# A scan and a mixture of adapters on one core: new orders for all engines, the sigmoid table first, 14 warm-up transposes

## The chip, the core and the metric

The kernel runs on one core of one Trainium2 chip. A core has five engines, each with an instruction queue of its own that is worked off strictly in order: TensorE (PE: matrix products and transposes), VectorE (DVE), ScalarE (ACT), GpSimd (POOL) and SyncE (SP), which here only issues DMAs. They meet through semaphores. Data comes from and goes to HBM through 16 DMA engines. The metric is the time of one execution in microseconds on the device; three runs of the kernel before gave 208.76, 209.05 and 209.07 us, median 209.05.

## What is computed

Two arrays `a` and `b` of 8 x 6400 x 128 (float32) are scanned along their second axis, and the result `x`, seen as 51200 rows of 128, passes through a mixture of eight low-rank adapters, of which each row takes two:

```python
h = a[:, t] * h + b[:, t]; x[:, t] = h          # for t in 0 .. 6399, h = 0 at the start

logits = x @ w_gate                              # 128 -> 8
topk = the two largest logits of each row
w = softmax of these two
out = x + sum over the two e of w_e * (x @ A[e]) @ B[e]     # 128 -> 16 -> 128
```

26.2 MB are read for `a`, as much for `b`, and 26.2 MB are written.

## The kernel before

The 51200 rows are cut into 100 chunks of 512 rows (`C`, line 148). `a` and `b` come by load DMAs (line 271) in pieces of one chunk (256 KB) for the first and the last four chunks and of four chunks (1 MB) between (`LOADS`, line 12), into four buffers `a_tm` and four `b_tm` of four chunks each. A buffer is loaded anew as soon as the transposes of its old chunks are done.

A chunk then passes through these steps; the letter is the one that stands for the step in the orders below:

- `a` on PE (line 308): four transposes of `a` into PSUM bank 0; `a` on ACT (line 321): the copy to `a_st`. There is one bank, so the next chunk's transposes wait for this copy.
- `b` on PE (line 308): four transposes of `b` into bank 1 or 2, where VectorE reads them.
- `s` on DVE (line 372): the scan along time, `x = a*x + b`, into `xT` in float16; the start value is the last column of the chunk before.
- `z` on PE (line 392): `x` times `A` and `w_gate` (128 x 136) for blocks of 128 rows; `z` on ACT (line 399): the copy of two or three blocks to `zl`.
- gating for a group of 1 to 6 chunks (`GROUPS`, line 14): `1 2 3 4 6` on DVE (lines 423 to 434) find the largest and the second largest logit, `5` on POOL (432) takes their difference, `u` and `v` on ACT (437, 439) its sigmoid with both signs, `p q r` on POOL (443 to 447) make the weights.
- `m` (line 469): the products with the weights, on POOL or DVE (`MU`, a letter for each chunk: `p` or `d`).
- `t` on PE (line 477): four transposes of them; `t` on ACT or DVE (lines 482, 483): the copy to `zwT` (`TE`, a letter for each chunk: `a` or `d`).
- `d` on PE (lines 491, 492): identity times `x` plus the products with `B`; `o` on ACT (line 502): the copy to `outt`.
- `o` on SP (line 528): the store DMA, one chunk (256 KB) for the first and last four chunks, two (512 KB) between: 54 stores.

On SP, `x` and `y` are the loads of `a` and of `b`; the very first `y` is issued by ACT, and so are the three loads of the constants (`c`, line 237). `w` on PE (line 241) are warm-up transposes of the identity matrix, whose results nobody uses; there are 30 (`WARM`), 16 of them ahead of the first chunk and the rest spread among the first chunks. `i` on ACT (line 238) is one sigmoid of a column, there to have its table loaded.

No scheduler decides the order: `ORDER` (lines 20 to 49) has one string for each engine, and `arrange` takes the steps of each letter in sequence. The waits follow from that order and the dependences. The numbers `dur=` beside the steps serve the search that made the strings; nothing on the chip reads them.

Of the kernel before, what the change touches and what calls it, by code (L numbers as in the profile page):

```python
# [18 lines left out]
WARM = 30  # L19
ORDER = {  # L20
    "pe": (
        "wwwwwwwwwwwwwwwwawwwwbawbwwzwzwwbazzwazabwwazabtzbwadbzazbzatbazbzazzbazbadbzatzbaztbadzztbazzbabztd"
        "bazdzbadzbazzbatzbaztzbadzbatdbzatzzdabbtzadtdzbabtzzadtdbadtzbatzbzabtdzzabdtazzdtbazdzbatzbzadtbaz"
        "dtbabdaztbzazdtazbzdbtadzztabztzddatbzzdtbabztdabdtzazbztazbddtadbzatdzztabdtabzbtadzztabzdtbzdatzdb"
        "atdbaztdazbzdaztbzdtbadztbzatzdbazdztbabdtazdtabzztbatzdadtzdzatbbadtzzdbtdazbtdzatdbazbztabzddtbzaz"
        "tddaztbbadtdzaztbbtzzdatadtbbdztdzabzzdabtzzatddzztdatbbtaddtzbzatdbatdazdtzabbtzadtbdzzbdaztzdaztdt"
        "zabtdabbztddztzbazdtbztzaddtbaztdbbztzadztzdtzdtdtzddttdtddttdtddtdd"
    ),
    "act": (
        "cyccaaizzzazvazavuuaatzazozazzatazzavzuazzaovuzaztaztazztaozzaztoavuzzazoazzatzazoazzoatzazuvoaotzaz"  # L30
        "tzaooazoozatuzazzvoazzaooazzatzzaooauzvzazoaooaztazzaozzoauzzozazvotoazzoazoaozaztazooazzuvaotazzoaz"
        "oazozzaooazoauvtzazoazozzaoozuaovzzatozzazaooazoaztvzazoauzzaooaotzotzavoozazoauzzatozozatzoatzouaov"
        "oazzztzaaoouozzaozzaovzzaoozzaotaozazoaoauvztaoozzoatozzazoozaztazvuooaztozztoazozzaotouuavozvzzaztz"
        "otootoutvzzoovuotovuootoooo"
    ),
    "dve": (
        "iscs1234s162346smmss1s2s132s34s46s6sss1s2s3s4s6sss1sst2s3s4st6s1ssts2t34sst6s1tsts23s4ststst1s263sst"
        "s4tst16tsstststss2346tstsstst1sts1t223t4s36s4ststststs1236st4ststsst6123t4tsmsms6tstss12st34ss6tstss"
        "1t2346tstsststttsstst123t4s6stssst12t34m6stssst1st1223344st66sts1m213m24346m6mtmt12m3m4tm6tmt"
    ),  # L40
    "pool": (
        "cc5q5ppqrr55qprmqpmrmm5qprmmmmmm5pqrmmmm5mmpqrmm5mmmmpqrmmm5mmmqprmmmmm5mqprmmmmmm5pqrmmm5mmmpqrm5mm"
        "mmm5qprmmmmpqrmm5mmmqprmm5mmmmqprmmmmmmm5pqrmmmm5mpqrmmmmm55mqpprmqr5q5prqpr5pqr"
    ),
    "sp": (
        "xxyyxxxyyxyxyxoyxyxyooxyxoyooxyyxxyooxoyyoxoxyoxyooxooyoxooyxoyooxyooxyooxoyoxoyooxoyooyyxxooxyyxooo"
# [4 lines left out]
    "aaaaaaadadaaddadddadddaddddadddaddadddddaddddadddadddaaddadaaddadddddddadddadaddadaaddaddaaaaddaddad"  # L51
)
MU = (
    "ddppppppppppppppppppppppppppppppppppppppppppppppppppppddpppppppppppppppppppppppppppdpppppppddddddddd"
# [80 lines left out]
def bass_associative_scan_2x2__then__mixture_of_adapters_kernel(  # L135
# [24 lines left out]
    seg_of = [s for s, m in enumerate(SEGMENTS) for _ in range(m)]  # L160
# [3 lines left out]
    with ExitStack() as stack:  # L164
# [53 lines left out]
        def dma_sem(key):  # L218
# [4 lines left out]
        o_ms = P.add("pool", "c", [], lambda: eng["pool"].memset(ident_f[:, :], 0.0), dur=0.2)  # L223
# [5 lines left out]
            ), dur=0.3,  # L229
# [8 lines left out]
        P.add("act", "i", [o_id], lambda: eng["act"].activation(tiny[:, :], ident_f[:, 0:1], ACTF.Sigmoid), dur=1.6)  # L238
        o_ih = P.add("dve", "i", [o_id], lambda: eng["dve"].tensor_copy(ident_h[:, :], ident_f[:, :]), dur=0.25)
        for k in range(WARM):  # L240
            w = P.add("pe", "w", [o_id], lambda: eng["pe"].transpose(ps[:, BANK_O[0], 0:128], ident_f[:, :], ident_f[:, :]),  # L241
                      dur=0.218 if k < 12 else 0.109)
            user[BANK_O[0]] = [w]
# [7 lines left out]
        tm_user = [[[None] * 4 for _ in range(NL)] for _ in range(2)]  # L251
        loads = []
        s, pos = 0, 0
        for n in LOADS:
            m = SEGMENTS[s]
            assert all(SEGMENTS[s + k] == m for k in range(n)) and pos % 4 + n * m <= 4
            loads.append((s, n, m, pos // 4 % NL, pos % 4))
            for k in range(n):
                place[s + k] = (pos // 4 % NL, pos % 4 + k * m)
            pos += n * m  # L260
            s += n
        assert s == len(SEGMENTS)

        def load(s, n, m, sl, q):
            P.at = first[s]
            for w, (o_l, tile, src) in enumerate(((o_la, a_tm, af), (o_lb, b_tm, bf))):
                e = "act" if s == 0 and w else "sp"
                old = [tm_user[w][sl][q + k] for k in range(n * m)]
# [7 lines left out]
                for k in range(n):  # L276
                    o_l[s + k] = op

        def landed(tile, s):

            sl, q = place[s]
            m = SEGMENTS[s]
            return tile[sl][:, q : q + m, :].rearrange("p h (j d) -> p (h j) d", d=D)


        o_A, o_B, o_ae, o_sc = {}, {}, {}, {}
        ast_user = [None] * NA
        x_user = [[] for _ in range(NX)]
        turn = {"a": 0, "b": 0, "z": 0}

        def front(s):
            m = SEGMENTS[s]
            sl, q = place[s]
            c0 = first[s]
            if m == 2 and turn["b"] % 2:
                turn["b"] += 1
            bk = bank(BANK_B, turn["b"])
            turn["b"] += m
            ab = c0 % NA
            xb = c0 % NX  # L300

            def trans(bk, tile, h):
                src = landed(tile, s)
                dv = ps[:, bk, :].rearrange("d (p k) -> d k p", k=4)

                def f():
                    for k in range(4):
                        last = eng["pe"].transpose(dv[:, k, :], src[:, m * k + h, :], ident_f[:, :])  # L308
                    return last

                return f

            o_ae[s] = []
            for h in range(m):
                P.at = c0 + h
                ba = bank(BANK_A, turn["a"])
                turn["a"] += 1
                o = P.add("pe", "a", [o_la[s], o_id] + user[ba], trans(ba, a_tm, h), dur=0.436)
                tm_user[0][sl][q + h] = o
                o2 = P.add("act", "a", [o, ast_user[ab + h]],  # L320
                           lambda h=h, ba=ba: eng["act"].copy(a_st[:, ab + h, :], ps[:, ba, :]), dur=0.589)  # L321
                user[ba] = [o2]
                o_ae[s].append(o2)
            if m == 2:
                tm_user[0][sl][q] = o
            bops = []
            for h in range(m):
                P.at = c0 + h
                o = P.add("pe", "b", [o_lb[s], o_id] + user[bk + h], trans(bk + h, b_tm, h), dur=0.436)
                bops.append(o)  # L330
            for h in range(m):
                tm_user[1][sl][q + h] = bops[-1]

            r0 = c0 * C
            n = m * C
            starts = sorted({0} | {k * S - r0 for k in range(NB) if 0 < k * S - r0 < n})
            cuts = list(zip(starts, starts[1:] + [n]))

            def timed(ap, s0, s1):

                if m == 1:
                    return ap[:, 0, s0:s1]
                return ap.rearrange("d h q -> d q h")[:, s0 // 2 : s1 // 2, :]

            def scan():
                for s0, s1 in cuts:
                    if (r0 + s0) % S == 0:
                        init = 0.0
                    elif s0:
                        raise AssertionError  # L350
                    else:
                        init = xT[:, (c0 - 1) % NX, C - 1 : C]
                    last = running(
                        timed(xT[:, xb : xb + m, :], s0, s1), timed(a_st[:, ab : ab + m, :], s0, s1),
                        timed(ps[:, bk : bk + m, :], s0, s1), init)
                return last

            o_sc[s] = P.add("dve", "s", o_ae[s] + bops + [o_sc.get(s - 1)] + [x for h in range(m) for x in x_user[xb + h]],
                            scan, dur=(1.276 if m == 1 else 2.343) + 0.16 * (len(cuts) - 1))
            for h in range(m):  # L360
                user[bk + h] = [o_sc[s]]
                ast_user[ab + h] = o_sc[s]
                x_user[xb + h] = [o_sc[s]]
# [3 lines left out]

        def running(out, data0, data1, init):

            v = eng["dve"]  # L370
            low = lambda ap: v.lower_ap(ap)
            return v.add_instruction(mybir.InstTensorScalarPtr(  # L372
                name=nc.get_next_instruction_name(), op0=ALU.mult, op1=ALU.add,
                is_scalar_tensor_tensor=True, is_tensor_tensor_scan=True,
                ins=[low(data0), v.lower_ap_or_imm(init) if isinstance(init, float) else low(init), low(data1)],
                outs=[low(out)]))
# [7 lines left out]
        def zlogits(b0, n):  # L384
# [10 lines left out]
            o = P.add("pe", "z", [o_sc[seg_of[(b0 + n - 1) // 4]], o_ch] + user[bk], zmm, dur=0.059 * n)  # L395
            for k in range(n):
# [3 lines left out]
                      dur=0.167 + 0.1133 * n)  # L400
# [54 lines left out]
        def back(gi, c, q0):  # L455
# [4 lines left out]
            m = SEGMENTS[seg_of[c]]  # L460
# [43 lines left out]
            for p in spots:  # L504
                out_user[p] = o_oe[c]
            while stored[0] < len(stores):
                s, n, m = stores[stored[0]]
                if first[s] + n * m > c + 1:
                    break
# [126 lines left out]
```

## Time and profile before

| what | value |
|---|---|
| median of three runs | 209.05 us |
| the profiled execution: its own time | 209.05 us |
| its span, first to last instruction | 207.2 us |
| moved by DMA | 79.18 MB, mean 382 GB/s |
| busiest engines | PE 193.4 us, ACT 184.7 us, DVE 180.3 us |
| granted TensorE clock | 0.996 |

The profile is one execution on the chip. Its views give the busy time of each engine, groups of instructions with their mean duration and what ended the idle time before them, the instructions in order of time, the DMA issues with the time until the data landed, and stretches of the run with the share of the 16 DMA engines that was busy. "SPq" and "ACTq" mark an engine's queue of DMA issues: their duration is how long the issue held the queue. L308 is line 308 of the kernel. Matrix products overlap in the pipeline, so that a busy PE is not one at its peak.

### The profile page before, as it was taken

The page shows a single profiled execution, that of the slowest core. Times are in us where ns is not written, and L with a number is a line of the kernel's source. Part 1 is how long each engine was busy: PE and PEld are TensorE (multiplying, and loading weights), DVE is VectorE, ACT ScalarE, POOL GpSimd, SP SyncE. Part 2 cuts the span into 40 slices and gives each one's busy share as a digit, 9 for nine tenths or more (in the row PEclk, how much of TensorE's full clock was granted, in tenths as well). Part 3 has the DMA queues.
Part 4 walks back from the last instruction along what each step waited for, and adds up shares of the span by engine and source line. Part 5 has one row for each costly group of instructions (what it writes and reads, how often), then busy time and mean ns, then how long its engine had stood idle before and what let it go on. Part 6 is the DMA issues. An engine that isn't in the chain of part 4 may idle for free.

```text
span 207.2 us, 6200 instructions
## 1 busy us (share of the span) xinstructions
PE 193.4 (93%) x2430; PEld 184.9 (89%) x2430; DVE 180.3 (87%) x297; ACT 184.7 (89%) x425; POOL 126.6 (61%) x184
## 2 busy tenths in 40 slices
PE   7969999999999999999999999999999999998760
PEld 7849889999999999999999999999899999996650
DVE  0579999999999998999999999998987899999930
ACT  2578899999999999999999999999898899999870
POOL 1020092676783788859678776788779775974310
PEclk9999999999999999999999999999999999999998
DMA  6999999999999999999999999999999999999993
GB/s 202 363 393 386 386 393 385 384 394 390 396 397 382 387 399 398 396 393 395 391 404 402 401 401 395 404 395 399 399 402 398 404 401 400 401 403 402 368 371 127
DMA packets 41613, 79.18 MB, mean 382 GB/s; under 512 B 3056, under 2 KB 3184, under 8 KB 41584
## 3 DMA queue, kind: packets, MB, share of 16 engines
q1 hardware_dynamic: 40112, 78.39, 100.2%
q10 hardware_dynamic: 1472, 0.40, 0.8%
q8 instruction: 19, 0.31, 0.6%
q14 instruction: 10, 0.08, 0.1%
HBM read 52.56 MB, written 26.21 MB: 380 GB/s over the span
## 4 chain that ended last, share of the span: by engine, by line
PE 74%; DVE 7%; ACT 6%; DMA 6%; issue 2%; POOL 1%; POOLq 0%
PE ps L308 36%; PE ps L392 10%; PE ps L477 9%; PE ps L491 8%; PE ps L492 8%; DMA a_tm<-in_a_dram 6%; DVE xT L372 4%; PE ps L241 2%; ACT a_st L321 2%; ACT zl L399 2%; ACT outt L502 2%; DVE zw L469 1%; DVE zwT L483 1%; POOL zw L469 0%; ACT zwT L482 0%
## 5 line engine op out<-in xcount | busy, mean ns | idle before, releaser
L372 DVE TENSOR_TENSOR_SCAN xT<-a_st,xT,ps 128x512 f16<-128x512 f32 x96 | 120.3, 1253 | 6.6 <-PE ps L308 3.4
L469 POOL TENSOR_TENSOR zw<-zl,g 128x512 f16<-128x512 f32 x86 | 90.8, 1077 | 10.7 <-PE ps L477 8.2
L321 ACT COPY a_st<-ps 128x512 f32<-128x512 f32 x100 | 61.1, 611 | 8.8 <-PE ps L308 8.4
L399 ACT COPY zl<-ps 128x408 f32<-128x408 f32 (+1 forms) x138 | 67.2, 519 | 1.4 <-PE ps L392 0.7
L308 PE MATMUL ps<-ident_f,a_tm 128*128 128x128 f32 x400 | 61.8, 277 | 1.3 <-ACT a_st L321 1.1
L502 ACT COPY outt<-ps 128x512 f32<-128x512 f32 x100 | 59.1, 615 | 2.6 <-PE ps L492 1.4
L308 PE MATMUL ps<-ident_f,b_tm 128*128 128x128 f32 x400 | 59.5, 275 | 0.0
L491 PE MATMUL ps<-ident_h,xT 128*128 128x128 f16 x400 | 54.4, 219 | 0.0
L492 PE MATMUL ps<-cst_h,zwT 128*128 128x128 f16 x400 | 54.2, 219 | 0.0
L308 PEld LDWEIGHTS ps<-ident_f,a_tm 128*128 128x128 f32 x400 | 43.9, 142 | 3.5 <-ACT a_st L321 1.3
L491 PEld LDWEIGHTS ps<-ident_h,xT 128*128 128x128 f16 x400 | 44.8, 113 | 1.0 <-ACT outt L502 0.7
L392 PE MATMUL ps<-cst_h,xT 128*128 128x136 f16 x400 | 43.4, 223 | 1.6 <-ACT a_st L321 0.7
L308 PEld LDWEIGHTS ps<-ident_f,b_tm 128*128 128x128 f32 x400 | 43.7, 142 | 0.3
L477 PE MATMUL ps<-ident_h,zw 128*128 128x128 f16 x400 | 38.7, 219 | 2.6 <-DVE zwT L483 1.7
L492 PEld LDWEIGHTS ps<-cst_h,zwT 128*128 128x128 f16 x400 | 39.2, 98 | 0.0
L392 PEld LDWEIGHTS ps<-cst_h,xT 128*128 128x128 f16 x400 | 32.3, 114 | 3.8 <-DVE xT L372 1.9
L432 POOL TENSOR_TENSOR dd<-m 128x24 f32<-128x24 f32 (+3 forms) x23 | 5.9, 258 | 42.6 <-DVE m L430 42.6
L477 PEld LDWEIGHTS ps<-ident_h,zw 128*128 128x128 f16 x400 | 27.1, 98 | 5.3 <-DVE zwT L483 2.3
L483 DVE COPY zwT<-ps 128x512 f16<-128x512 f16 x62 | 25.4, 410 | 3.5 <-PE ps L477 3.2
L482 ACT COPY zwT<-ps 128x512 f16<-128x512 f16 x38 | 23.2, 611 | 0.2
L445 POOL TENSOR_TENSOR g<-k,w 128x192 f32<-128x192 f32 (+3 forms) x23 | 9.8, 428 | 11.3 <-ACT w L439 5.1
L443 POOL TENSOR_TENSOR t<-k,w 128x192 f32<-128x192 f32 (+3 forms) x23 | 10.1, 442 | 4.6 <-ACT w L437 4.5
(23 smaller groups left out, 89.8 us busy)
## 6 DMA issues: line engine op xcount, KB each, us to landing
a_tm<-in_a_dram SPq DMA_DIRECT2D x23, 1024.0 KB, 13.2
b_tm<-in_b_dram SPq DMA_DIRECT2D x23, 1024.0 KB, 13.9
out_dram<-outt SPq DMA_DIRECT2D x46, 512.0 KB, 11.9
a_tm<-in_a_dram SPq DMA_DIRECT2D x8, 256.0 KB, 7.5
out_dram<-outt SPq DMA_DIRECT2D x8, 256.0 KB, 7.9
b_tm<-in_b_dram SPq DMA_DIRECT2D x7, 256.0 KB, 10.1
b_tm<-in_b_dram ACTq DMA_DIRECT2D x1, 256.0 KB, 4.2
cst_f<-in_moe_A_dram ACTq DMA_DIRECT2D x1, 64.0 KB, 3.3
```

Source lines behind the costliest of these rows:

```text
L308: last = eng["pe"].transpose(dv[:, k, :], src[:, m * k + h, :], ident_f[:, :])
L321: lambda h=h, ba=ba: eng["act"].copy(a_st[:, ab + h, :], ps[:, ba, :]), dur=0.589)
L372: return v.add_instruction(mybir.InstTensorScalarPtr(name=nc.get_next_instruction_name(), op0=ALU.mult, op1=ALU.add, is_scalar_tensor_tens ...
L392: last = eng["pe"].matmul(ps[:, bk, k * W : k * W + W], xblock(b0 + k), Awg_h)
L399: lambda: eng["act"].copy(zl[:, z0 : z0 + n, :].rearrange("p k w -> p (k w)"), ps[:, bk, 0 : n * W]),
L469: lambda: eng[me].tensor_tensor(out=wv, in0=zv, in1=gv, op=ALU.mult),
L477: last = eng["pe"].transpose(pT[:, k * 128 : k * 128 + 128], zw[w][:, k, :], ident_h[:, :])
L482: f = (lambda: eng["act"].copy(zwT[w][:, :], pT[:, 0:512])) if te == "act" else (lambda: eng["dve"].tensor_copy(zwT[w][:, :], pT[:, 0:512]))
L483: lambda: eng["dve"].tensor_copy(zwT[w][:, :], pT[:, 0:512]))
L491: eng["pe"].matmul(dst, xblock(b0 + k), ident_h[:, :], start=True, stop=False)
L492: last = eng["pe"].matmul(dst, zwT[w][:, k * 128 : k * 128 + 128], B_h, start=False, stop=True)
L502: lambda: eng["act"].copy(place_o, ps[:, bo, :].rearrange("p (k d) -> p k d", d=D)), dur=0.578)
```

## The change

The five strings and `TE` and `MU` are replaced by others, found with other durations for the steps (ACT copies 0.59 to 0.60 instead of 0.578 to 0.589, the first two chunks' transposes longer by 1.95 and 1.3, and so on). The number of warm-up transposes goes from 30 to 14; two stand ahead of the first chunk. The sigmoid's activation is made a condition of the first copy on ACT and stands ahead of it. ACT issues its load of `b` ahead of the first constant instead of behind it. TE goes from 38 copies on ACT and 62 on DVE to 33 and 67, MU from 86 products on POOL and 14 on DVE to 90 and 10. The scan is written with the language's own instruction instead of one put together by hand, the same in the built program. Code for half-chunk loads is added that `SEGMENTS`, unchanged, does not use.

```diff
-WARM = 30
+WARM = 14
+COLD, SOLO, FUSED = {0: 1.95, 1: 1.3}, 0.872, 0.95
 ORDER = {
     "pe": (
-        "wwwwwwwwwwwwwwwwawwwwbawbwwzwzwwbazzwazabwwazabtzbwadbzazbzatbazbzazzbazbadbzatzbaztbadzztbazzbabztd
+        "wwbawwwwawbzzazzwbwawwwawwbaazbzzbatzbazztabdabzadbabzzatbzazbzatbzazzdtabtbaddzazbzabzdaztbaztbzdtb
...
     "act": (
-        "cyccaaizzzazvazavuuaatzazozazzatazzavzuazzaovuzaztaztazztaozzaztoavuzzazoazzatzazoazzoatzazuvoaotzaz
+        "yccciaazzazzaauvvuazazzaztazzaoatuvaozazvuazzazzaztaztazovaouzazzazoatzaozzotazzazozaozavuztaztzzoao
...
-        "otootoutvzzoovuotovuootoooo"
+        "ozvvuuoozototuvootoooo"
     "dve": (
-        "iscs1234s162346smmss1s2s132s34s46s6sss1s2s3s4s6sss1sst2s3s4st6s1ssts2t34sst6s1tsts23s4ststst1s263sst
+        "iscs1234612346ssss1s213243s46s6sstsss1234s6stsssts1s2s3ts4s6ss1ststs2s34st6stsss1s2s3t4st6sst1ststst
...
-        "1t2346tstsststttsstst123t4s6stssst12t34m6stssst1st1223344st66sts1m213m24346m6mtmt12m3m4tm6tmt"
+        "tst123t46ststststst1st234s6tstsstst1234t6mtssstst1s1t223344t6s6mmsts1122334466tmtmt12m3m46mtmt"
...
     "sp": (
-        "xxyyxxxyyxyxyxoyxyxyooxyxoyooxyyxxyooxoyyoxoxyoxyooxooyoxooyxoyooxyooxyooxoyoxoyooxoyooyyxxooxyyxooo
+        "xxyxxyxyyxyxyxxyoooyxyxooyxyxyxooyoxoyxoyoooxoyyxxyyoxooxoyooxoyoxyoxoyoooyxooyxooxooyoxoxyoyoxxyoyo
         "ooooooooooooooo"
...
-        P.add("act", "i", [o_id], lambda: eng["act"].activation(tiny[:, :], ident_f[:, 0:1], ACTF.Sigmoid), dur=1.6)
+        o_sg = P.add("act", "i", [o_id], lambda: eng["act"].activation(tiny[:, :], ident_f[:, 0:1], ACTF.Sigmoid), dur=1.6)
...
+        def emptied(c):
+            ab = c % NA
+            ba = bank(BANK_A, c)
+            o_ae[c] = P.add("act", "a", [o_A[c], ast_user[ab], o_sg if c == 0 else None],
+                            lambda: eng["act"].copy(a_st[:, ab, :], ps[:, ba, :]), dur=0.602)
+            user[ba] = [o_ae[c]]
```

How the steps around the first stores stand on three engines, each numbered by its own letter from 0 (SP's `y0` is chunk 1's load, as ACT issues chunk 0's; from `x4` and `y3` on a load holds four chunks):

```
before  SP   ... x6 y5 x7 o0 y6 x8 y7 x9 y8 o1 o2 x10 ...
after   SP   ... x6 y5 x7 x8 y6 o0 o1 o2 y7 x9 y8 x10 o3 o4 ...
after   ACT  ... a15 z16 t2 a16 z17 t3 a17 z18 o2 v4 a18 o3 ...
after   PE   ... z16 b13 a16 z17 z18 d2 t4 a17 b14 t5 b15 a18 ...
```

And SP's end:

```
before  SP   ... x29 y28 y29 x30 o36 o37 ... o53
after   SP   ... x29 x30 y28 o37 y29 o38 o39 ... o53
```

More of the change, by code (lines that the diff above doesn't have):

```diff
@@ L221, in dma_sem @@
             return key
[L223 removed]
+        o_ms = P.add("pool", "c", [], lambda: eng["pool"].memset(ident_f[:, :], 0.0), dur=0.46)
         o_id = P.add(
@@ L287, in bass_associative_scan_2x2__then__mixture_of_adapters_kernel, with used @@
+        def used(w, c, o):
+            sl, q, m, h = place[c]
+            for k in range(m):
+                tm_user[w][sl][q + k].append(o)
+        o_ae, o_sc = {}, {}
         ast_user = [None] * NA
         x_user = [[] for _ in range(NX)]
[L289 to L343, printed above, removed]
@@ L356, in scan @@
-                return last
[L358 to L363, printed above, removed]
+                    init = 0.0 if (r0 + s0) % S == 0 else xT[:, (c - 1) % NX, C - 1 : C]
```

173 lines of the change are left out of this document (98 added, 75 removed).

## The prediction

> **What bounds the kernel now.** I read the page first, then SyncE's DMA issues in order of time, then the stretches of the run, then the last store. The page:
>
> ```profile
> span 207.2 us, 6200 instructions
> PE 193.4 (93%) x2430; PEld 184.9 (89%) x2430; DVE 180.3 (87%) x297; ACT 184.7 (89%) x425; POOL 126.6 (61%) x184
> GB/s 202 363 393 386 386 393 385 384 394 390 396 397 382 387 399 398 396 393 395 391 404 402 401 401 395 404 395 399 399 402 398 404 401 400 401 403 402 368 371 127
> q1 hardware_dynamic: 40112, 78.39, 100.2%
> q8 instruction: 19, 0.31, 0.6%
> PE 74%; DVE 7%; ACT 6%; DMA 6%; issue 2%; POOL 1%; POOLq 0%
> ```
>
> Two readings compete. The chain (last line) names TensorE, and three engines are near 90% busy: a compute-bound kernel. But SyncE's queue q1 holds the 16 DMA engines for 100.2% of the span, and the bandwidth stands near 400 GB/s from the third slice to the 37th. Which one ends the run shows in how SyncE issues:
>
> ```profile
> 5.79 2.94 SPq L271 DMA_DIRECT2D b_tm<-in_b_dram  x1
> ...
> 13.86 2.58 SPq L271 DMA_DIRECT2D a_tm<-in_a_dram  x1
> 20.06 0.36 SPq L528 DMA_DIRECT2D out_dram<-outt  x1
> 20.46 0.86 SPq L271 DMA_DIRECT2D b_tm<-in_b_dram  x1
> ```
>
> An issue that costs 0.36 us when there is room costs 2.58 to 2.94 us here. That is the time in which one 1 MB load passes (1.049 MB at 390 GB/s, 2.7 us): the issue is held until the queue has room, so the DMA engines have work in stock. How much, the landings tell (all loads of `a`):
>
> ```profile
> DMA to landing us min/median/max: 2.7/12.6/15.8
> ```
>
> 2.7 us is a load into an empty queue, 12.6 the usual one: some 10 us of work stand ahead of a transfer. Between 16.44 (13.86 + 2.58) and 20.06 SyncE waited 3.6 us for the first store's copy, and the next slices kept their 386 GB/s. Waits of that size are hidden. By stretches (last two columns: share of the 16 engines, GB/s):
>
> ```profile
> 2.00:20.00 18.00, 15.81 (x125) 14.40 (x125) 10.97 (x21) 11.24 (x25) 1.71 (x8) 1.00 1.05 369
> 160.00:194.00 34.00, 32.45 (x432) 30.16 (x430) 31.40 (x64) 33.03 (x82) 23.54 (x37) 1.00 1.05 401
> 194.00:200.00 6.00, 4.93 (x77) 4.12 (x74) 4.76 (x14) 4.77 (x13) 1.74 (x7) 1.00 0.92 351
> ```
>
> The share is 1.05 until 194 us and falls only in the last 6 us of compute. There the stores come as fast as ScalarE makes them, and some DMA engines have nothing. The last store and what follows it:
>
> ```profile
> L528 SPq DMA_DIRECT2D out_dram<-outt x1: 382/382/382, 201.1 to 201.1; - x1
> DMA to landing us min/median/max: 5.6/5.6/5.6
> ```
>
> ```profile
> 203.00:204.00 1.00, 0.00 (x0) 0.00 (x0) 0.00 (x0) 0.00 (x0) 0.00 (x0) 1.00 0.41 154
> 204.00:205.00 1.00, 0.00 (x0) 0.00 (x0) 0.00 (x0) 0.00 (x0) 0.00 (x0) 1.00 0.17 66
> 205.00:206.00 1.00, 0.00 (x0) 0.00 (x0) 0.00 (x0) 0.00 (x0) 0.00 (x0) 0.69 0.07 27
> ```
>
> It lands 5.6 us after its issue, not 2.7. At 400 GB/s one of 16 engines moves 25 GB/s, so 66 and 27 GB/s are two to three engines, then one. These lag behind the others and still have a backlog of 5.6 - 2.7 = 2.9 us. So I read the end as set by **the most loaded DMA engine**, busy from 2 us to 206 us without a gap, and compute as having 2.9 us of room at its last store. Orders on the compute engines cannot shorten that engine's work; they can only starve it.
>
> **The change, part by part.** Bytes, number of DMAs and their sizes stay, and so do all matrix, scan and gating instructions, so the terms below are those of compute and of order.
>
> ```profile
> 2.82 1.28 ACT L321 ACT_TABLE_LOAD   x1 [2.82 <-issue]
> ...
> 6.09 0.59 ACT L321 COPY a_st<-ps 128x512 f32<-128x512 f32 x1 [1.99 <-PE ps L308]
> ...
> 8.73 1.28 ACT L238 ACT_TABLE_LOAD   x1
> ...
> 10.02 0.20 ACT L238 ACTIVATE tiny<-ident_f 128x1 f32<-128x1 f32 x1
> ...
> 11.25 0.59 ACT L321 COPY a_st<-ps 128x512 f32<-128x512 f32 x1
> ```
>
> Table first: the load at 2.82 becomes the sigmoid's and its 0.20 us activation stands behind it; ready at 4.3 us, before the first copy has anything to copy (6.09 in this run). The load at 8.73 goes, with the activation after it: 1.28 + 0.20 = 1.5 us less on ScalarE among the first copies. On the end: 0, since DMA's stock covers the first 20 us.
>
> ```profile
> 1.53 3.67 PE L241 MATMUL ps<-ident_f 128*128 128x128 f32 x16 [1.53 <-POOL ident_f L226]
> ```
>
> ```profile
> 5.00 1.06 PE L308 MATMUL ps<-ident_f,a_tm 128*128 128x128 f32 x4
> ...
> 8.03 0.60 PE L308 MATMUL ps<-ident_f,b_tm 128*128 128x128 f32 x4
> ```
>
> ```profile
> b_tm<-in_b_dram ACTq DMA_DIRECT2D x1, 256.0 KB, 4.2
> ```
>
> Warm-ups: 16 go, and only 2 instead of 16 stand ahead of the first real transposes, which here run at 1.06 us per four and from 8 us on at 0.60, after some six us of work. Now TensorE stands idle from 2.0 us until the first `b` lands (its load needs 4.2 us here and moves to the head of ScalarE's queue, one constant's issue of about 0.5 us earlier, so at 4 to 5; the constants behind it keep their places but one), so `b0, a0, a1, b1` may all cost 1.06: 2 x 0.46 = 0.9 us more at worst for chunk 1; at best nothing, as the 16 ahead also delayed `a0`. I take 0.5 us late at the first scans, against 1.5 won on ScalarE; both die in the stock. The Trainium skill ("TensorE: Matmul & The Clock Gate", Part 1: The HAM clock gate) says that the array runs at half clock until a window of about 3.4 us was busy, and this speaks against the cut: by it the cold stretch, estimated, ends one window after the work becomes dense, near 8 us, about where it ends now. The granted-clock column is 1.00 throughout, and only the durations show the step.
>
> ```profile
> L482 ACT COPY zwT<-ps 128x512 f16<-128x512 f16 x38 | 23.2, 611 | 0.2
> ```
>
> ```profile
> L483 DVE COPY zwT<-ps 128x512 f16<-128x512 f16 x62 | 25.4, 410 | 3.5 <-PE ps L477 3.2
> L469 DVE TENSOR_TENSOR zw<-zl,g 128x512 f16<-128x512 f32 x14 | 9.7, 702 | 0.4 <-POOL g L447 0.3
> ```
>
> Who copies and multiplies: counting letters, TE goes from 38 `a` and 62 `d` to 33 and 67, MU from 14 `d` and 86 `p` to 10 and 90. ScalarE: -5 x 0.611 = -3.1 us, with the table -4.5. VectorE: +5 x 0.410 - 4 x 0.702 = -0.8. GpSimd takes four multiplies more, out of its 39% of idle time. None of it on the path: 0.
>
> The searched orders: they move every engine's work, but what counts is SyncE's, because there a wait holds all loads behind it. Two places are tighter than before.
>
> (1) The third store. Before, SyncE has 9.4 MB of loads out when it first waits for a store. After, two 1 MB loads more come ahead (11.5 MB), then three stores in a row, and every further load waits behind the third. The last of the 9.4 MB landed at 13.9 + 15.8 = 29.7:
>
> ```profile
> L271 SPq DMA_DIRECT2D a_tm<-in_a_dram x1: 2577/2577/2577, 13.9 to 13.9; - x1
> ...
> DMA to landing us min/median/max: 15.8/15.8/15.8
> ```
>
> Two loads (5.4) and two 256 KB stores (1.3) more: the stock lasts to 36.4. The third store's copy stands behind the `a` copies of chunks 16 and 17, and chunk 16 is in that very load of 29.7.
>
> ```profile
> L399 ACT COPY zl<-ps 128x408 f32<-128x408 f32 (+1 forms) x138 | 67.2, 519 | 1.4 <-PE ps L392 0.7
> L321 ACT COPY a_st<-ps 128x512 f32<-128x512 f32 x100 | 61.1, 611 | 8.8 <-PE ps L308 8.4
> L502 ACT COPY outt<-ps 128x512 f32<-128x512 f32 x100 | 59.1, 615 | 2.6 <-PE ps L492 1.4 <-DMA out_dram<-outt 1.1
> ```
>
> From 29.7: transposes 0.6, then `a` 0.61, `z` 0.52, `t` 0.61, `a` 0.61, `z` 0.52, `o` 0.62, together 4.1: 33.8. A transfer needs about 2.0 us from its issue to its first bytes (2.7 less the 0.7 that 256 KB takes), so the store feeds the queue at 35.8, and the load behind it 0.4 later. Margin 0.6 us: no gap, but little room, where the first wait before had 29.7 - 20.1 - 2.0 = 7.6.
>
> (2) The last load. After it 16 stores follow instead of 18, two of 512 KB less: it lands 2 x 1.3 = 2.6 us later than before.
>
> ```profile
> L271 SPq DMA_DIRECT2D a_tm<-in_a_dram x1: 469/469/469, 174.9 to 174.9; - x1
> ...
> DMA to landing us min/median/max: 10.2/10.2/10.2
> ```
>
> Before: 185.1, and the last store is issued 16.0 us later. If that distance stayed, the last store would come at 203.7 and, into an empty queue, land at 206.4; the lagging engine ends at 206.7 anyway. And the distance shrinks: behind the last scan VectorE has 6 multiplies instead of 9. So 0.
>
> **Sum:** 207.2 + 0, and 1.85 us around the span as in the profiled execution (209.05, which is also the median of the three runs): **209.0 us**.
>
> **Rivals.** *(A) Compute is the bound after all, or the lagging engine lags less: faster.* For it: the chain's 74% TensorE and the 4.5 us less on ScalarE. Against: a share of 1.05 to 194 us and held issues. What is to be had is the 2.9 us of the last store's backlog, if compute also ends no later: 206.2 to 208.6, say 207.7. One way there: an instruction fetch less on that engine. The q8 row gives 0.006 x 16 x 207.2 / 19 = 1.05 us per packet; the Trainium skill ("Runtime: NRT & Kernel Launch", Instruction fetch mechanics) says that instructions come in blocks of 256, so that the 32 TensorE instructions that go (16 transposes, a weight load each) would be an eighth of one, at most one packet, and it calls the cost mostly hidden, where the trace has it on the engines that carry the data.
>
> *(B) The third store starves DMA: slower.* It decides if that copy ends after 34.4 instead of 33.8, because TensorE's order puts a transpose and four matmul pairs ahead of chunk 17's transposes, or the cold start was not made up by then. Each us beyond is a us on the end, to about 2: 209.6 to 211.
>
> *(C) Compute's tail outgrows its room: slower.* Decides if the last store is issued after 204.0; 0.5 to 1.5 us: 209.5 to 210.5. Against it: the three multiplies fewer.
>
> That the change does not do what it says I leave out: in the built program one table load is left, ahead of the copies.
>
> **How the numbers follow.** Forecast 0.42 (its own range 208.6 to 209.4), A 0.28, B 0.20, C 0.10. A change of 0.2% (0.4 us) is about what a measurement can tell from none. Faster 0.28, same 0.42, slower 0.30. The range reaches into A to 207.5 and into B to 210.3: beyond lie the outer parts of A (about 0.1) and B (0.08).
>
> **What would show it.** Right: share 1.05 in all stretches to about 190, issues of 2.5 us and more, one table load, the last store landing near 206.7 with one or two engines left over. (1) wrong: a fall of GB/s between 34 and 38 us, and a landing of under 4 us for the load behind the third store. (2) wrong: last store after 204. A shorter span with the same share up to 190 and a quicker fall after 203 would be A. The early parts are right if the `a` copies of chunks 2 to 5 come earlier than 11.25 us and on, without a change of the end.

## The result, and the profile after

The changed kernel is slower: 210.72 us in the median (209.95 to 210.91, four executions) against 209.05, a ratio of 1.0076 with a 95% interval of 1.0048 to 1.0104. The forecast was 209.0 with a range up to 210.3. On another chip, beside two experiments, it took 210.11 (209.82 to 210.87, six executions), 1.0063 (1.0042 to 1.0083). So the loss is real and between 0.9 and 2.2 us. All times here are of fast executions; two executions of one version below, with the fourth store ahead, took 391 and 496 us and are left out. The profiled execution is the 209.95 one, and its span is 1.0 us longer than that of before. Lines from its page:

```profile
span 208.2 us, 6169 instructions
...
PE 190.9 (92%) x2414; PEld 182.8 (88%) x2414; DVE 180.8 (87%) x298; ACT 182.0 (87%) x419; POOL 131.0 (63%) x188
...
GB/s 204 356 394 387 384 385 328 377 375 405 385 386 390 406 397 391 403 401 392 385 388 398 406 398 406 398 398 394 401 400 400 400 403 402 402 407 402 379 368 134
...
q1 hardware_dynamic: 40112, 78.39, 99.9%
...
PE 42%; DMA 39%; ACT 6%; DVE 5%; SPq 4%; issue 1%
DMA b_tm<-in_b_dram 25%; PE ps L287 20%; DMA a_tm<-in_a_dram 14%; PE ps L463 6%; PE ps L477 5%; PE ps L478 5%; PE ps L379 5%; SPq L272 4%; DVE xT L349 2%; ACT outt L485 2%; ACT zl L386 2%; ACT a_st L315 1%; ACT zwT L468 1%; DVE zwT L469 1%; DVE zw L455 1%
```

Work went down on TensorE (193.4 to 190.9 us) and ScalarE (184.7 to 182.0), bytes are the same, and the run is longer. Two things are new. The chain of waits, three quarters TensorE before, runs for 39% through transfers. And the bandwidth has one dent in its plateau: the seventh slice, 31 to 36 us, has 328 GB/s where before had 385. The stretches of that place, first of before and then of the changed kernel (length, then busy us and number of instructions of PE, of its weight loads, of VectorE, ScalarE and GpSimd, the granted clock, the busy share of the 16 DMA engines and the GB/s):

```profile
34.00:36.00 2.00, 2.00 (x27) 1.84 (x25) 2.00 (x5) 2.00 (x6) 0.00 (x0) 1.00 1.05 387
36.00:38.00 2.00, 2.00 (x28) 2.00 (x26) 2.00 (x4) 2.00 (x7) 0.31 (x2) 1.00 1.04 386
38.00:40.00 2.00, 2.00 (x26) 2.00 (x25) 1.87 (x2) 1.96 (x5) 1.84 (x4) 1.00 1.05 382
```

```profile
32.00:34.00 2.00, 2.00 (x27) 1.91 (x26) 1.90 (x5) 2.00 (x6) 0.24 (x1) 1.00 1.05 393
34.00:36.00 2.00, 2.00 (x28) 1.94 (x26) 2.00 (x4) 2.00 (x6) 1.00 (x2) 1.00 0.71 236
36.00:38.00 2.00, 2.00 (x28) 2.00 (x26) 1.90 (x3) 1.98 (x5) 1.89 (x3) 1.00 1.04 354
38.00:40.00 2.00, 2.00 (x27) 1.93 (x25) 1.79 (x2) 2.00 (x6) 2.00 (x3) 1.00 1.01 379
...
160.00:194.00 34.00, 32.55 (x436) 30.76 (x435) 32.51 (x66) 32.75 (x81) 24.62 (x36) 1.00 1.05 402
```

The engines of compute are as busy in 34 to 36 us as before; only the DMA engines have a hole. Taken from the plateau's 1.05, the three stretches lack (0.34 + 0.01 + 0.04) x 2 = 0.78 us of the time of all 16 engines. From 40 us on the shares are level with those of before again. What SyncE did there, in order of time (start, duration):

```profile
19.89 2.75 SPq L272 DMA_DIRECT2D b_tm<-in_b_dram  x1
22.69 11.30 SPq L508 DMA_DIRECT2D out_dram<-outt  x3
34.03 0.43 SPq L272 DMA_DIRECT2D b_tm<-in_b_dram  x1
34.51 1.15 SPq L272 DMA_DIRECT2D a_tm<-in_a_dram  x1
```

The three stores are one row of 11.3 us, most of it the wait for the third; the next load goes out at 34.03, right behind the third store at 33.65. It is place (1) of the prediction. In half microseconds the hole has two parts, one before the third store's data and one between these and the load's:

```profile
33.50:34.00 0.50, 0.50 (x12) 0.50 (x10) 0.50 (x1) 0.50 (x3) 0.00 (x0) 1.00 1.05 401
34.00:34.50 0.50, 0.50 (x12) 0.50 (x10) 0.50 (x2) 0.50 (x2) 0.00 (x0) 1.00 0.66 234
34.50:35.00 0.50, 0.50 (x9) 0.50 (x7) 0.50 (x2) 0.50 (x3) 0.04 (x1) 1.00 0.92 307
35.00:35.50 0.50, 0.50 (x7) 0.43 (x6) 0.50 (x1) 0.50 (x2) 0.50 (x2) 1.00 0.90 287
35.50:36.00 0.50, 0.50 (x8) 0.50 (x7) 0.50 (x2) 0.50 (x2) 0.46 (x1) 1.00 0.37 115
36.00:36.50 0.50, 0.50 (x8) 0.50 (x6) 0.50 (x2) 0.50 (x2) 0.47 (x1) 1.00 1.11 336
```

At the end, the stretch after compute and the last two stores (issue times, then the time to landing):

```profile
203.00:208.00 5.00, 0.00 (x0) 0.00 (x0) 0.00 (x0) 0.00 (x0) 0.00 (x0) 0.61 0.35 135
```

```profile
L508 SPq DMA_DIRECT2D out_dram<-outt x2: 332/332/332, 201.9 to 202.4; - x2
...
DMA to landing us min/median/max: 5.2/5.2/5.3
```

The last store is issued at 202.4 (201.1 before) and lands 5.2 us later: a lagging DMA engine still ends the run, one microsecond later than before.

### The profile page after: what moved, and what is told of

It is laid out like the page before. It is cut to its first block, busy times and chain, and to the rows that moved or that the text cites. A ratio compares the mean times of both kernels' runs of the same rounds, so it can differ in the third digit from the quotient of the medians.

```text
span 208.2 us, 6169 instructions
## 1 busy us (share of the span) xinstructions
PE 190.9 (92%) x2414; PEld 182.8 (88%) x2414; DVE 180.8 (87%) x298; ACT 182.0 (87%) x419; POOL 131.0 (63%) x188
## 4 chain that ended last, share of the span: by engine, by line
PE 42%; DMA 39%; ACT 6%; DVE 5%; SPq 4%; issue 1%
DMA b_tm<-in_b_dram 25%; PE ps L287 20%; DMA a_tm<-in_a_dram 14%; PE ps L463 6%; PE ps L477 5%; PE ps L478 5%; PE ps L379 5%; SPq L272 4%; DVE xT L349 2%; ACT outt L485 2%; ACT zl L386 2%; ACT a_st L315 1%; ACT zwT L468 1%; DVE zwT L469 1%; DVE zw L455 1%
## 5 line engine op out<-in xcount | busy, mean ns | idle before, releaser
L455 POOL TENSOR_TENSOR zw<-zl,g 128x512 f16<-128x512 f32 x90 | 93.6, 1062 | 9.8 <-PE ps L463 8.2
L287 PE MATMUL ps<-ident_f,b_tm 128*128 128x128 f32 x400 | 61.1, 278 | 4.4 <-DMA b_tm<-in_b_dram 4.3
L379 PE MATMUL ps<-cst_h,xT 128*128 128x136 f16 x400 | 42.6, 224 | 0.8 <-DVE xT L349 0.6
L463 PEld LDWEIGHTS ps<-ident_h,zw 128*128 128x128 f16 x400 | 27.8, 98 | 4.5 <-DVE zwT L469 1.1
L469 DVE COPY zwT<-ps 128x512 f16<-128x512 f16 x67 | 27.3, 408 | 2.9 <-PE ps L463 2.6
L468 ACT COPY zwT<-ps 128x512 f16<-128x512 f16 x33 | 20.2, 613 | 1.5 <-PE ps L463 1.3
L432 POOL TENSOR_TENSOR g<-k,w 128x192 f32<-128x192 f32 (+3 forms) x23 | 10.4, 451 | 4.6 <-DVE k L421 2.3
```

Of the source, the lines that this page charges most:

```text
L287: return [lambda k=k: eng["pe"].transpose(dv[:, k, :], src[r, k, :], ident_f[r, r]) for k in range(4 * m)]
L379: last = eng["pe"].matmul(ps[:, bk, k * W : k * W + W], xblock(b0 + k), Awg_h)
L455: lambda: eng[me].tensor_tensor(out=wv, in0=zv, in1=gv, op=ALU.mult),
L463: last = eng["pe"].transpose(pT[:, k * 128 : k * 128 + 128], zw[w][:, k, :], ident_h[:, :])
L468: f = (lambda: eng["act"].copy(zwT[w][:, :], pT[:, 0:512])) if te == "act" else (lambda: eng["dve"].tensor_copy(zwT[w][:, :], pT[:, 0:512]))
L469: lambda: eng["dve"].tensor_copy(zwT[w][:, :], pT[:, 0:512]))
```

## The experiments

Theory: the third store's wait runs the queue dry, and what the DMA engines miss there comes back at the end. Rivals: the new orders of the compute engines cost the time, or the start (table, warm-ups) does, or the end is not set by the DMA engines at all.

### One letter: the third store behind two more loads

The changed kernel, with one place of SyncE's order altered:

```diff
-        "xxyxxyxyyxyxyxxyoooyxyxooyxyxyx...
+        "xxyxxyxyyxyxyxxyooyxoyxooyxyxyx...
```

> The changed kernel with one letter of SyncE's order moved: the third store stands behind two more 1 MB loads (o0 o1 y7 x9 o2 instead of o0 o1 o2 y7 x9). Stock theory (the wait for the third store's copy let most DMA engines run empty near 34 to 37 us; they lost their lead over the slowest one, and later hits by instruction fetches, which that lead had hidden, then count): 209.0 to 209.5, no dip near 34 to 38 us, the lead of the fastest engines at the load behind the third store still about 2 us. Tail theory (the last loads come 2.6 us later and compute ends later): no change from the changed kernel, 210.5 to 210.9. Compute theory (the new orders or the missing warm-ups cost engine time): the same, 210.5 to 210.9.

Measured: 209.07 us (208.66 to 209.28), ratio to before 1.0003 (0.9989 to 1.0017). The hole is gone:

```profile
34.00:36.00 2.00, 2.00 (x30) 1.94 (x28) 2.00 (x3) 2.00 (x6) 0.71 (x2) 1.00 1.05 396
36.00:38.00 2.00, 2.00 (x28) 2.00 (x26) 1.90 (x4) 1.98 (x6) 1.84 (x3) 1.00 1.04 391
38.00:40.00 2.00, 2.00 (x27) 1.93 (x25) 1.80 (x2) 2.00 (x5) 2.00 (x3) 1.00 1.05 383
```

```profile
23.51 4.03 SPq L508 DMA_DIRECT2D out_dram<-outt  x2
27.58 0.64 SPq L272 DMA_DIRECT2D b_tm<-in_b_dram  x1
28.26 2.58 SPq L272 DMA_DIRECT2D a_tm<-in_a_dram  x1
33.98 0.36 SPq L508 DMA_DIRECT2D out_dram<-outt  x1
34.38 1.28 SPq L272 DMA_DIRECT2D b_tm<-in_b_dram  x1
```

The third store is issued at 33.98, no earlier than in the changed kernel (33.65); compute is the same. Only the two loads at 27.58 and 28.26 are new ahead of it. That one letter is worth the whole loss.

### SyncE's order of before in the changed kernel

`ORDER["sp"]` of before, all else changed.

> The changed kernel with SyncE's order of before, all other orders as changed. Stock and tail theory both: 208.9 to 209.4. Compute theory: 210.5 to 210.9.

Measured: 208.94 us (208.67 to 209.43), ratio 1.0001 (0.9987 to 1.0015). The new orders of PE, ACT, DVE and POOL, the table and the 14 warm-ups together give and cost nothing. The profiled execution (208.67 us) shows how much room there is: TensorE was busy for 0.58 of the 4 us from 104 to 108, the granted clock was 0.66 in the next four, the last store went out at 202.9 instead of 201.1 and landed 3.5 us later, and the run is no longer than before.

### SyncE's new order in the kernel before

> The kernel before with SyncE's order of the changed one, all other orders as before. Stock theory: the third store's copy comes at 34.6 us by the order of before, one us later than in the changed kernel, so the dip is deeper: 210.5 to 212. Tail theory: 210 to 210.9. Compute theory: 209.0.

Measured: 211.32 us (210.85 to 211.76), ratio 1.0111 (1.0085 to 1.0136). The one string alone brings a loss, and a larger one. With the old compute orders the third store goes out at 34.4:

```profile
34.00:36.00 2.00, 0.83 (x8) 0.83 (x9) 0.49 (x3) 1.15 (x3) 0.00 (x0) 1.00 0.67 234
36.00:38.00 2.00, 2.00 (x28) 2.00 (x27) 2.00 (x3) 1.68 (x4) 0.23 (x1) 1.00 0.91 276
38.00:40.00 2.00, 2.00 (x28) 2.00 (x27) 2.00 (x3) 1.93 (x6) 0.75 (x2) 1.00 1.01 356
```

The hole is (0.38 + 0.14 + 0.04) x 2 = 1.12 us, and here compute stands still, too, in 34 to 36 us (VectorE 0.49 of 2 us). At the end it is compute that is late. The last five stores:

```profile
L528 SPq DMA_DIRECT2D out_dram<-outt x5: 332/345/372, 202.7 to 205.7; - x5
...
DMA to landing us min/median/max: 3.1/3.2/3.6
```

The last store goes out at 205.7 (201.1 before) and lands 3.1 us later. The first DMA engine is done 0.8 us ahead of the last, in the kernel before 3.2, so no backlog to speak of is left. So this run shows that the string alone does harm; its 2.4 us are not the price of the hole through the DMA engines alone.

### Table and warm-ups alone

The kernel before with its own orders, but for the head of them:

```diff
-WARM = 30
+WARM = 14
-    "pe":  "wwwwwwwwwwwwwwwwawwwwbawb...
+    "pe":  "wwawwbawb...
-    "act": "cyccaaizzz...
+    "act": "yccciaazzz...
-                o2 = P.add("act", "a", [o, ast_user[ab + h]],
+                o2 = P.add("act", "a", [o, ast_user[ab + h], o_sg if c0 + h == 0 else None],
```

> The kernel before with two parts of the change alone: the sigmoid's table and activation ahead of the first copy (and the load of b ahead of the constants), and 14 warm-ups, two of them ahead of the first chunk. Stock and tail theory: 208.8 to 209.4, as the first 20 us are covered by loads in stock. Compute theory: 209.8 to 210.7.

Measured: 208.95 us (208.69 to 209.35), ratio 0.9999 (0.9984 to 1.0014). The first scan of its profiled execution starts at 6.64 us, that of before at 7.69:

```profile
6.64 1.22 DVE L372 TENSOR_TENSOR_SCAN xT<-a_st,ps 128x512 f16<-128x512 f32 x1 [4.90 <-PE ps L308]
```

```profile
7.69 1.22 DVE L372 TENSOR_TENSOR_SCAN xT<-a_st,ps 128x512 f16<-128x512 f32 x1 [5.96 <-PE ps L308]
```

That is no quicker start: in two later runs that have the head of before unaltered (the one without four stores and the one with split stores, below) the first scan starts at 6.56 and 6.85. The 7.69 belongs to the one profiled execution of before, whose transposes ran at the slow rate for longer (the last section). Either way nothing of it reaches the end.

### A larger hole

The changed kernel, with the fourth store ahead of the loads as well:

```diff
-        "xxyxxyxyyxyxyxxyoooyxyxooyxyxyx...
+        "xxyxxyxyyxyxyxxyooooyxyxoyxyxyx...
```

> The changed kernel with one letter of SyncE's order moved the other way: the fourth store, too, stands ahead of the loads that wait behind the third. In the changed kernel the third store's copy ends at 33.6 us and the next o copy of ScalarE runs from 34.17 to 34.76, so the first load behind the stores goes out near 35.2 instead of 34.03, 1.15 us later, with 256 KB (0.65 us) more of its own in the queue. Theory (what the DMA engines could not move from 34 us on comes back as time at the end, one for one): the stretch 34 to 38 us loses 0.2 to 0.45 MB more than in the changed kernel, so +0.5 to +1.15 us: 211.2 to 211.9 us. Rival (the loss at the third store is harmless, the whole cost comes from what the loads behind it meet later, a fetch on an engine that lost its lead): no more than the changed kernel's 210.7, give or take 0.3, as the later fetches are the same.

```profile
34.00:36.00 2.00, 2.00 (x27) 1.94 (x25) 2.00 (x5) 2.00 (x7) 1.11 (x3) 1.00 0.80 285
36.00:38.00 2.00, 2.00 (x29) 2.00 (x28) 1.90 (x2) 1.98 (x6) 1.92 (x3) 1.00 0.75 221
38.00:40.00 2.00, 2.00 (x27) 1.93 (x25) 1.79 (x3) 2.00 (x5) 2.00 (x3) 1.00 0.94 336
```

The hole grew to (0.25 + 0.30 + 0.11) x 2 = 1.32 us, and behind it compute stood still, too (TensorE was busy for 0.90 of the 2 us from 42 to 44, and the granted clock fell to 0.56 in the next two). But the time was 210.72 us, ratio 1.0081 (1.0063 to 1.0099), the changed kernel's own. That spoke for the rival. The intervals were too wide to hold 0.5 us apart, so both kernels ran again side by side.

> The changed kernel unaltered, beside the next two on one chip, for a comparison with more executions of each. In its trace the stretch 34 to 40 us moved 0.40 MB less than in the version with the third store behind two loads (1.0 us at 395 GB/s), and its time was 1.6 us above the 209.07 of that version. Both theories expect 210.7, give or take 0.2.

> The version with the fourth store, too, ahead of the loads; its trace lost 0.65 MB (1.65 us at 395 GB/s) in 34 to 40 us, and three executions gave 210.72. If what is lost on the mean over 16 engines comes back one for one: 0.65 us above the changed kernel beside it (211.3). If the price is set by the one engine that ends last, and that engine had a lead of its own to spend first: within 0.3 us of the changed kernel beside it.

Measured: the changed kernel 210.11 us, ratio 1.0063 (1.0042 to 1.0083); with the fourth store ahead 211.18 us, ratio 1.0102 (1.0086 to 1.0118). The intervals lie apart, though barely; the medians differ by 1.1 us. So in this comparison a larger hole costs more, and the idea that a lead absorbs it does not hold. The size of the step isn't settled: 0 us in the first comparison, which was not side by side, 1.1 us in the second.

### A smaller step: one load ahead of the third store

```diff
-        "xxyxxyxyyxyxyxxyoooyxyxooyxyxyx...
+        "xxyxxyxyyxyxyxxyooyoxyxooyxyxyx...
```

> The changed kernel with the third store behind one more 1 MB load only (it needs 2.65 us of the DMA engines). The stretch 34 to 36 us lost 0.32 MB in the changed kernel, 0.8 us; one load of stock more than covers it. If the loss of stock at this place is the whole cause: no fall of GB/s between 34 and 40 us and 209.0 us, give or take 0.3. If the order of the two loads and later stores against each other matters by itself (the place of the store among the loads, not the stock): about half way, 209.6 to 210.2.

Measured: 209.12 us (208.98 to 209.59), ratio 1.0011 (1.0001 to 1.0021), beside the 210.11 of the changed kernel. One letter has moved by one place; the hole is gone and nearly all of the loss:

```profile
34.00:36.00 2.00, 2.00 (x27) 1.93 (x25) 2.00 (x5) 2.00 (x7) 1.13 (x3) 1.00 1.08 412
```

| version | hole in 34 to 40 us (of all engines) | above before, us |
|---|---|---|
| third store behind two loads | 0.02 | 0.15 |
| third store behind one load | 0 | 0.14 |
| changed kernel | 0.78; 0.90 | 1.67; 1.13 |
| before with the new SyncE order (compute ends it) | 1.12 | 2.40 |
| fourth store ahead, too | 1.32 | 1.75; 2.20 |

The holes are read from one execution each, the differences are those of medians on one chip; the second value of the changed kernel is that of the repeated run (shares of 0.72, 0.95 and 1.03). By these medians a hole of x us came back as 1.3 to 2.1 x. Set against the time of the very execution that the hole was read from (209.95, 210.23 and 210.54 us, 0.90, 1.25 and 1.57 above before), and leaving out the version that compute ends, it came back as 1.2 to 1.4 x.

### Is the end set by the DMA engines?

The kernel before without four of its stores in mid-run (chunks 36 to 43), whose rows are not written; SyncE's string has four letters `o` fewer:

```diff
-                store(s, n, m)
+                if not 20 <= stored[0] < 24:
+                    store(s, n, m)
```

> The kernel before without four of the stores in mid-run (chunks 36 to 43, 2 MB of the 26.2 MB written; these rows are not written). Compute is the same. If the DMA engines' total is the bound all through and compute follows the data: 2.1 MB at 400 GB/s is 5.2 us, so 203.8 us. If compute ends where it ends now (last store at 201.1) and only the lagging engine's 2.9 us of backlog go: 206.1. If compute is the bound (TensorE's 74% of the chain): 208.9, no change.

Measured: 205.85 us (205.72 to 206.00), ratio 0.9848 (0.9835 to 0.9861): 3.1 us less with the same compute. It is the middle case. The last two stores:

```profile
L529 SPq DMA_DIRECT2D out_dram<-outt x2: 332/369/406, 200.1 to 200.6; - x2
...
DMA to landing us min/median/max: 2.7/2.8/2.8
```

They go out half a microsecond before those of before, and land after 2.8 us instead of 5.6: the backlog of the lagging engine is gone, and compute is what remains, 3 us below. The share tells the same:

```profile
160.00:194.00 34.00, 32.40 (x433) 30.07 (x431) 31.79 (x66) 32.81 (x82) 24.02 (x39) 1.00 0.97 369
194.00:200.00 6.00, 5.13 (x76) 4.32 (x76) 4.26 (x12) 4.94 (x11) 1.37 (x6) 1.00 0.72 268
```

So the kernel before is bound by its DMA engines with 3 us to spare in compute, and rival (A), compute as the bound, is out.

### Three that decide nothing

The kernel before, with the constant `A` brought in long runs:

```diff
-   ("ca", 0.94, cst_f[:, 0:128].rearrange("p (e r) -> p e r", e=E), moe_A.rearrange("e d r -> d e r")),
+   ("ca", 0.94, cst_f[:, 0:128], moe_A.rearrange("e (h j) r -> (e h) (j r)", j=8)),
```

> The kernel before with one thing changed: the constant A comes in 128 runs of 512 B instead of 1024 runs of 64 B; its elements then stand in another arrangement than the products need, which this run leaves out. In the trace of before the 64 B packets took 11 ns each, 10.9 us together, and the 512 B packets of the other constant 27 ns: 10.9 us becomes 3.5 us, 0.47 us for each of 16 engines, all of it at the start. If the DMA engines are the bound from 2 us to the end: 0.4 to 0.5 us less, 208.5. If the one engine that ends last is held by something else (its fetches, the late stretch), or compute is the bound: no change, 208.98 give or take 0.15.

Measured: 208.73 us (208.51 to 209.49) against 209.06, ratio 0.9989 (0.9977 to 1.0000). That is 0.2 us less by the ratio and 0.3 by the medians, where 0.4 to 0.5 were expected, with an interval that holds both the 0.45 us and nothing.

Two late stores split by partitions, so that the 16 engines are loaded otherwise:

```diff
+SPLIT = (84, 86)
+            parts = ((0, 120), (120, 128)) if s in SPLIT else ((0, 128),)
+            for lo, hi in parts:
+                    lambda lo=lo, hi=hi: eng["sp"].dma_start(dst[lo:hi], src[lo:hi]),
```

> The kernel before with two of the late stores (chunks 84 to 87) each issued as two DMAs of 120 and of 8 partitions; the same bytes go. A DMA of 120 partitions leaves the division among the 16 engines another than one of 128. If one fixed engine is the one that lags at the end, and it is the one relieved by this division: up to 64 KB less on it, 1.3 us at 25 GB/s per two stores: 207.6 to 208.3. If the one relieved is another: 208.9, give or take 0.2; if the small DMAs all fall on the lagging engine: up to 210.2. The theory that the end is set by one lagging engine expects any of these but shows itself by a change in the last 3 us of the run; the rival that all engines end together by chance expects no change in the order of landings.

Measured: 209.28 us (209.04 to 209.83), ratio 1.0017 (1.0009 to 1.0026), 0.3 us more. The last store was issued at 202.4 instead of 201.1, though its copy was done no later (at 200.8 us, before at 201.1), so the split delayed the stores behind it, and this hides which engine was relieved. (The 1.3 us of the expectation is what 32 KB take at 25 GB/s; 64 KB would take 2.6.)

More instructions to fetch on SyncE, in the version with the third store behind two loads:

```diff
-            for op in P.order[name]:
+            for n, op in enumerate(P.order[name]):
+                if name == "sp" and n >= 25:
+                    for _ in range(30):
+                        handle.wait_ge(s_eng["pe"], 1)
```

> The changed kernel with the third store behind two more loads (209.07 us), and 30 waits that are satisfied already ahead of each SyncE instruction from the 26th on, some 2700 instructions more on SyncE and nothing else; the data moved and the compute are the same. Theory (instruction packets take their time on the DMA engines that carry the data, 1.05 us each of one engine, and the lagging one pays): the row of instruction packets grows from 19 by about 10, and the end comes 0.6 to 1.5 us later: 209.7 to 210.6. Rival (fetches are hidden by the queues' stock): 209.1, give or take 0.2. SyncE's own time for the waits may delay issues; if issues stay held by the queue (2.5 us and more a piece), that is not the cause.

Measured: 216.43 us (216.09 to 216.56), ratio 1.0351 (1.0337 to 1.0365), far beyond both. The end of its issues shows why:

```profile
100.00:160.00 60.00, 57.19 (x756) 55.47 (x755) 54.50 (x85) 53.74 (x123) 42.80 (x54) 1.00 1.04 388
160.00:194.00 34.00, 31.94 (x420) 30.24 (x419) 30.02 (x54) 30.03 (x71) 24.04 (x33) 1.00 0.98 352
```

In the last stretch the DMA engines stood empty part of the time: 30 waits took 0.9 us ahead of each issue (stores that cost 0.38 us followed each other at 1.3), and SyncE came late with the loads. The ten more instruction packets are there (row q14 of the page has 20 instead of 10), but the late issues hide their price. It tells of late issues once more, and nothing of the fetches it was made for.

## Why the prediction was wrong, point by point

**What bounds the kernel: right.** The DMA engines, with some 3 us of room in compute: 2 MB less took 3.1 us off, and the last store's landing fell from 5.6 to 2.8 us.

**Table, warm-ups, who copies: right.** All together are worth 0.0 us (208.94 against 208.92). The sign for the early parts, `a` copies of chunks 2 and on earlier than 11.25 us, came (10.06 and 11.96 for chunks 2 and 3, 11.25 and 12.65 before), but it proves nothing: in the run without four stores, with the head of before, they start at 10.12 and 11.52. The two scans that the forecast had 0.5 us late start at 6.89 and 9.06, against 7.69 and 9.05 in the profile of before, but 6.56 and 7.91 in that run, and 6.85 and 8.20 in the one with split stores. Against these the first scan comes 0 to 0.3 us late and the second about one: the late start was there, hidden by a chance of the one profiled execution of before.

**Place (1), the third store: the step that failed** is "the stock lasts to 36.4 ... Margin 0.6 us: no gap, but little room". The times in it were right: the third store was forecast for 33.8 and went out at 33.65, the second store landed at 36.51, 12.0 us after its issue at 24.55. What was wrong is what a landing says. A DMA counts as landed when the slowest of its 16 engines has finished. At the landing of 36.51 the first engine was 2.1 us ahead of that one, the eighth 1.8 and the fifteenth 1.0. The stock of the first engine therefore ended at 34.4 and that of the eighth at 34.7, not at 36.4, and against the 35.8 at which the third store was to feed the queue the margin was not +0.6 but -1.4 us for the first and -1.1 for the eighth. The times at which each of the 16 engines had finished its part are in the trace; worked out from them, for the DMA that landed next to the time on the left (when the first and the eighth engine were done, and the last):

```
            before                 changed                third store behind two loads
near        first  eighth last     first  eighth last     first  eighth last
30 us       28.44  28.65  30.30    27.82  28.05  29.83    28.11  28.31  30.16
36 us       33.71  33.97  35.62    34.44  34.72  36.51    34.14  34.46  36.19
43 us       41.82  42.07  43.69    41.45  41.94  42.56    40.77  41.09  42.81
59 us       56.96  57.28  58.88    57.02  57.49  59.00    58.76  59.08  60.80
```

In all three kernels fifteen engines lead the last by 1.5 to 2 us from 24 to 30 us; then some of them fall back, and the first eight keep their lead. The landings also tell what the engines missed in the changed kernel. The first engine finished the second store at 34.44, the third at 35.64 and the load behind it at 38.78; with some 0.65 us of work in the store and 2.7 in the load it stood empty for some 0.55 us before the store and 0.45 before the load, the eighth for 0.4 and 0.8. So the store's bytes came sooner than the forecast's 35.8 and the load's later than 0.4 us behind them, and only the sum, 1.0 to 1.2 us, is near the margin.

In the changed kernel the hole takes the lead to 1.1 us (first) and 0.6 us (eighth) at 43 us, while the last engine shows no hole: against before at the same number of bytes it was 0.1 to 0.3 us late there. The lead is back at 59 us, and by then the last engine is late itself: 0.9 us at 48.6 us and 1.2 at 56. (From 102 to 121 us the difference is 0.3 us or less, since before has such a step of its own at 98.7; from 124 us on it is 0.9 to 1.5, and 1.0 when the run ends. The first engine's is 1.0 us at 39 and 1.0 to 1.5 from then on.) So the loss was not paid when it arose, and a look at the last landing alone (5.9 us for the load behind the store, not the "under 4 us" that was to show it) would have missed it.

How the others' loss passes to the one that ends last is argued, not shown: an engine that serves an instruction fetch stops for one microsecond, and when its lead is gone, it becomes the last. The traces fit this, but do not name the engine that serves a fetch. In the trace of before such a fetch starts at 19.83 and takes 1.11 us, and the lead of the other engines grows from 0.4 us at the landing of 20.09 to 1.9 at the next, 24.23. In the changed kernel a fetch starts at 42.95, when the first engine's lead is 1.1 us, and the last engine falls back by 0.7 us at the next landing, 45.95; a fetch at 43.4 in the other two kernels of the table, where that lead is 1.9 to 2.1, leaves no such step. The run that should have tested it told nothing. The Trainium skill ("Runtime: NRT & Kernel Launch", Instruction fetch mechanics) calls the cost of crossing from one block of instructions to the next mostly hidden. That is said of the engine that runs the instructions; what the landing of 24.23 shows is a cost on the DMA engines that carry the data.

**Rival (B): right in its place, wrong in its point of decision.** It was to decide if the copy ended "after 34.4 instead of 33.8". The copy came in time by that mark, at 33.6, and the queue ran dry all the same. Its price, 209.6 to 211, holds: 210.1 and 210.7. Of the two signs named for it, the fall of GB/s between 34 and 38 us came (236 in 34 to 36). The chance of 0.20 came from that margin. With the lead taken off, (B) would have been the forecast.

**Place (2), the end: right as to its sign.** The last load goes out at 178.3 and lands 10.6 us later, at 188.9, 3.8 us later than before (2.6 forecast; the rest, 1.2 us, is about what the last engine is late by then). The last store follows it after 13.5 us instead of 16.0, so the distance shrank as forecast, and the last store's issue at 202.4 stays below the 204.0 at which rival (C) would have begun.

## What to carry to other kernels

Where transfers are the bound, count the stock of a DMA queue to the first of its engines that runs empty, not to the landing of the last: the two lay 2 us apart here, and that was three times the margin that the forecast saw. A wait in a queue that issues loads must be covered by loads ahead of it, and one load moved one place decides it. Less work on engines with room, 2.5 us on TensorE and 2.7 on ScalarE, buys nothing.

## What the runs showed of the hardware

- The 16 DMA engines drift apart: the first one led the last by 0.4 us at 20 us, 1.9 at 30 and 5.8 at 188 in the kernel before, and the average share stays at 1.05 all the while.
- A hole of 0.8 to 1.3 us in the average of the engines' work cost 1.1 to 2.2 us at the end by the medians, and 0.9 to 1.6 in the very executions that the holes were read from: somewhat more than the hole itself.
- The first transposes of the changed kernel ran at the slow rate longer than to the 8 us estimated for them (start, duration of four):

```profile
7.96 1.06 PE L287 MATMUL ps<-ident_f,b_tm 128*128 128x128 f32 x4
...
10.77 0.60 PE L287 MATMUL ps<-ident_f,b_tm 128*128 128x128 f32 x4
```

  TensorE's real work began at 4.2 us, and the slow rate lasted to 9.0 us at least. That step moves from execution to execution: with the 16 warm-ups of before, which begin at 1.5 us, the rate rose near 7.5 us in the profiled execution of before, but in the runs without four stores and with split stores the four transposes of the first chunk took 0.60 us already at 4.8. So the prediction's "after some six us of work" was read from a single execution. The Trainium skill ("TensorE: Matmul & The Clock Gate", Part 1: The HAM clock gate) has a window of about 3.4 us that must be busy, and says that it does not start with the kernel. The 3.3 and 6 us between the first warm-up and the step agree with that, the longer one being less than two such windows. It cost nothing, as the start was covered.
- A wait that is satisfied already still takes SyncE about 30 ns; 30 of them ahead of every issue from the 26th on cost 7.4 us of the run.
